# An adaLN block whose first layer norm of groups 2 and 3 is applied to a copy of x laid out by features

## Chip, cores and metric

The kernel runs on one core of one Trainium2 chip. The metric is the device time of one execution in microseconds (us). The time before is 711.41 us, the median of 3 runs (711.18 to 713.69).

## What is computed

A block with adaptive layer norm: sliding-window attention (16 heads of 28, window 256), then a dense layer, Mish, and a dense layer. S = 2048 tokens, D = 448 features, F = 1792.

```python
mod = (silu(c) @ w_mod).reshape(1, 6, 1, 448)      # sa, ca, ga, sb, cb, gb
h = layernorm(x) * (1 + ca) + sa
q, k, v = split(h @ wqkv)                          # 16 heads of 28
p = softmax(mask(q @ k.T / sqrt(28)))              # 0 <= i - j < 256
x = x + ga * ((p @ v) @ wo)
h = layernorm(x) * (1 + cb) + sb
x = x + gb * (mish(h @ w1 + b1) @ w2)
```

## The kernel before

Every matmul operand is split into a high and a low part (hi = value rounded by the write to the matmul type, lo = value - hi), and a product is summed from hi x hi, hi x lo and lo x hi. So each tile that TensorE (PE) makes is evicted twice: ScalarE (ACT) writes hi, VectorE (DVE) writes lo.

The 2048 tokens are four groups of 512 (NG = 4, GT = 512). For each group the first layer norm (L272 to L278, gen_ln at L226) works by tokens: x is loaded with tokens on partitions (x_load, L105), DVE takes mean and variance of each of four tiles (L220, L221), GpSimd (POOL) makes (variance + eps)^-0.5 (L234, L235), DVE subtracts and scales (L241), POOL copies 64 columns once more (dup, L224). Then gen_hT (L287) turns it to features on partitions: four chunks of four PE transposes (L250) into a PSUM buffer "mm", ACT writes hh = chunk * (1 + ca) + sa (L257), DVE makes the same sum in PSUM (L254) and writes hl (L262). From hh and hl come q and k tiles (stored to DRAM through scr) and v.

Attention runs in units. A slot is one head of one group; it has three units, so a group has 48 units: group 0 has units 0 to 47, group 1 has 48 to 95. In unit u (loop at L1026) PE does, in this order: the product of V with Pl of unit u-3 (L741), the scores sB of unit u (L709, L720), score maxima sA for a later slot (L679, reduced by DVE at L681, two PSUM buffers), some filler, and the product of V with Ph of unit u-2. ACT makes P and Ph by exponentials (L723, L724), POOL makes Pl = P - Ph (L731); P, Ph and Pl have three buffers each. The maxima of a pair of slots are transposed (mt, L687), split by DVE (mr, L690) and sent into the q tile by DMA (q<-mr). Every second slot has an et transpose block (L755).

Filler is other work fed to the engines a step at a time by two generators of a group: fill_main (PE work: qkv tiles of this and the next group, the output projection of the group before, gen_hT of the next group) and fill_side (gen_ln1 of the next group, then the preparation of modulation vectors: gen_mod_wo in group 0, gen_mod_ln2 in groups 1 and 2). Each unit adds RATE[g] to a credit and takes filler until it is used up; what is left is drained at the next group's start. The side generator is stepped once per unit; it names "dve" or "act" before a step that uses that engine, and is then passed over in some units (L1064).

All DMAs are issued by SyncE (SP) in one order; a transfer that has to wait for a buffer or for data holds those behind it. DMAs of the filler go into a list, later, from which most units issue one. Every engine works through its own queue in the order of the program.

Of the kernel before, what the change touches and what calls it, by code (L numbers as in the profile page):

```python
# [48 lines left out]


@with_exitstack
def adaln_block(ctx: ExitStack, tc: tile.TileContext, x, wqkv, wo, w1, b1, w2, c, w_mod, out):
# [5 lines left out]
    def dma(o, i):  # L58
        nc.sync.dma_start(o, i)
# [28 lines left out]
    scr = dram.tile([2 * D, 3, S], F32, name="scr")  # L88
    x1d = dram.tile([S, D], F32, name="x1d")
    xnd = dram.tile([NG - 1, GT, 512], F32, name="xnd")  # L90

    def bank(tag, bufs, name):
        return PS[0].tile([128, 512], F32, name=name, tag=tag, bufs=bufs)


    xin = {}

    def x_tile(g):
        xin[g] = qk.tile([128, 4, 512], F32, name=f"xin{g}", tag="xin")

    def x_half(g, t):
        r = g * GT + t * 128
        dma(xin[g][:, t:t + 2, 0:D], xf[r:r + 256, :].rearrange("(t p) d -> p t d", p=128))

    def x_load(g):  # L105
        x_tile(g)
        x_half(g, 0)
        x_half(g, 2)

    x_load(0)  # L110
    wm01 = []
    for k in range(4):
        wmf = st0.tile([128, 2 * D], F32, name=f"wm01_{k}")
# [112 lines left out]
    def gen_ln(tiles, pl, xn_tiles, key, mv=None):  # L226
        if mv is None:
            mv = pl.tile([128, 4, 2], F32, name=f"mv{key}", tag="mv", bufs=2)
            for t in range(4):
                ln_stats(tiles[t], mv[:, t, :], pl, f"{key}{t}")  # L230
                if t < 3:
                    yield
        rs = pl.tile([128, 4], F32, name=f"rs{key}", tag="rs", bufs=2)
        POOL.tensor_scalar(rs, mv[:, :, 1], EPS, None, op0=ALU.add)  # L234
        POOL.tensor_tensor(rs, rs, mhalf, op=ALU.pow)  # L235
        yield
        yield
        xs = xn_tiles()
        for t in range(4):
            xn = xs[t]  # L240
            DVE.tensor_scalar(xn[:, 0:D], tiles[t], mv[:, t, 0:1], rs[:, t:t + 1],  # L241
                              op0=ALU.subtract, op1=ALU.mult)
            if t:
                dup(xs[t - 1])
            yield xs
        dup(xs[3])
# [22 lines left out]
    done = set()  # L269
    XS, HT = {}, {}  # L270

    def gen_ln1(g):  # L272
        def xn_tiles():
            return [xin[g][:, t] for t in range(4)]
        for r in gen_ln([xin[g][:, t, 0:D] for t in range(4)], qk, xn_tiles, f"a{g}"):
            if r:
                XS[g] = r
            yield "dve"  # L278


    def cost(n, cols):
        return n * max(cols / 2200, 0.107)

    pipe = Pipe()
    ht_done = set()

    def gen_hT(g):  # L287
        drain(ln1[g])
        hh, hl = HT[g] = new_T(g, mid)
        for ci in range(4):  # L290
            p = bank("mm", 2, f"tr{g}{ci}")
            tr_chunk(XS[g], ci, p)
            pipe.add(2, lambda p=p, ci=ci: hT_hi(p, ci, hh, 0), lambda p=p, ci=ci: hT_lo(p, ci, hh, hl, 0))
            yield 1.2
        ht_done.add(g)
        if g + 1 < NG:
            loads = (lambda: x_load(g + 1),) if g > 1 else (lambda: (x_tile(g + 1), x_half(g + 1, 0)),
                                                            lambda: x_half(g + 1, 2))
            pipe.add(0, None, None, lambda: later.extend(loads))

    def finish():
        while pipe.items:
            yield
# [1 line left out]
    def drain(*gs):  # L305
        for g in gs:
            for _ in g:
                pipe.step()

    chunk = {"v": 4}  # L310

# [85 lines left out]
    xs0 = XS[0] = [xin[0][:, t] for t in range(4)]  # L397
    for t in range(4):
        ln_stats(xs0[t][:, 0:D], mv0[:, t, :], qk, f"a0{t}")
        if t % 2:  # L400
# [48 lines left out]
    first_split(1)  # L449
    for i in range(2):  # L450
        mod_cols_out(pm[:, 4 * i:4 * i + 4], i)
    hh, hl = HT[0] = new_T(0, mid)
    for ci in range(4):
        hT_hi(trs[ci], ci, hh, 0)
        if ci % 2:
# [40 lines left out]
            for f in qk_out(0, m, p):  # L496
                f()

    x_load(1)
# [25 lines left out]
    wol = [mid.tile([128, D], F32R, name=f"wol_{i}", tag="wo", bufs=7) for i in range(3)]  # L525

    def xr_tile(name):
        return mid.tile([128, 512], F32, name=name, tag="xr", bufs=3)


    def stg(pl, name):
        return pl.tile([128, 512], F32, name=name, tag="stg", bufs=4)

    def wm_load(i, k, pl, ws):
        ws.append(stg(pl, f"wm{i}_{k}")[0:112, 0:D])
# [244 lines left out]
    def lazy(f):  # L780
        yield from f()
# [154 lines left out]
    def fill_main(g):  # L936
        if g == 0:
            yield from gen_qkv(0, VT[:2] + (1,) + VT[2:] + (5, 2, 6))
        else:
            yield from gen_qkv(g, (5, 2, 6))  # L940
            if g == NG - 1:
# [15 lines left out]
    def fill_side(g):  # L957
        if g + 1 < NG:
            yield from ln1[g + 1]
            while g + 1 not in ht_done:  # L960
# [19 lines left out]
    ln1 = {g: gen_ln1(g) for g in range(1, NG)}  # L980
    fillers = {g: fill_main(g) for g in range(NG)}
    side = {g: fill_side(g) for g in range(NG)}

# [3 lines left out]
    def need(keys, g):  # L987
        if all((g, m) in done for m in keys):
            return
        flush()  # L990
        while not all((g, m) in done for m in keys):
            pipe.step()
            try:
# [32 lines left out]
    for u in range(NU + 9):  # L1026
# [27 lines left out]
        if g < NG:  # L1054
            v = u - 48 * g
            if v in (0, 12):
                chunk["v"] = 4 if v == 0 and g or 0 < g < NG - 1 else 2
            if v == 0:
                credit = 0.0
            credit += RATE[g] * (2 if v < FRONT[g] else 1)  # L1060
            while credit > 0.0:
                credit -= step(g)
            if v > 1 or g == 0:
                side_step(g, ("dve", "act")[a >= NS:] if k == 1 else ("act",) if k == 0 and s % 2 == 0 else ())  # L1064
            if later and ((s + (k == 2)) % 2 == 0 or k == 1):
                later.pop(0)()
        if u == NU:
# [111 lines left out]
        st.close()  # L1179


_INS = ["A_x", "A_wqkv", "A_wo", "B_w1", "B_b1", "B_w2", "c", "w_mod"]
_OUTS = [((1, S, D), "float32")]


# [17 lines left out]
```

## Time and profile before

| | |
|---|---|
| runs | 711.41 us median (711.18 to 713.69) |
| profiled execution | 710.72 us |
| its span, first to last instruction | 708.9 us |
| DVE, ACT, POOL busy | 54%, 55%, 46% of the span |
| granted TensorE clock | 0.998 |
| L250 on x (gen_hT) | 48 transposes, from 53.4 to 277.1 us |

The profile is of one execution. Busy is the time in which an engine has an instruction at work; PE's instructions overlap, so PE's place for an instruction is the distance between the starts of two. In rows of the timeline, a bracket tells how long the engine sat idle before the instruction and what ended that. Names are those of the program without buffer numbers; "pv<-Pl" is the product of V with Pl.

The unit at L1026 can be found in the trace by the starts of sB: unit 48 (the start of group 1) starts at 121.6 us, unit 96 at 223.1 us.

### The profile page before, as it was taken

The numbers are of one execution on the slowest core, as the hardware profiler recorded it, in microseconds if no ns is written. First come the engines' busy times: TensorE is split into PE (matmuls) and PEld (weight loads), VectorE is DVE, ScalarE is ACT, GpSimd is POOL, SyncE is SP. The second block draws the span as 40 slices with busy tenths as digits, with TensorE's granted clock in tenths as the row PEclk, the third lists the DMA queues.
The fourth block names the chain that finished last, engine by engine and source line by source line (L and its number), as shares of the span: only waits on it lengthen the run. The fifth ranks groups of instructions, "written<-read, shape, count | busy, mean of one in ns | idle before, by whom it ended". The sixth has DMA issues, their size and how long they took to land.

```text
span 708.9 us, 12034 instructions
## 1 busy us (share of the span) xinstructions
PE 686.6 (97%) x4001; PEld 589.5 (83%) x4001; DVE 385.2 (54%) x1031; ACT 391.1 (55%) x740; POOL 327.0 (46%) x358
## 2 busy tenths in 40 slices
PE   9899999999999999999999799999999999999996
PEld 8677788888898788898887688888888888888885
DVE  5588667688664888555768744351324332532112
ACT  3628778767766858767877874343223322422221
POOL 6626779586766777666778947222010000000002
PEclk9999999999999999999999999999999999999999
DMA  7865764454662462763774155810250035001001
GB/s 211 253 226 181 226 198 150 137 161 150 192 216 66 153 207 76 195 200 92 226 216 128 54 192 166 228 29 1 104 119 1 0 104 119 1 12 41 1 1 52
DMA packets 75178, 90.16 MB, mean 127 GB/s; under 512 B 31535, under 2 KB 51741, under 8 KB 75117
## 3 DMA queue, kind: packets, MB, share of 16 engines
q1 hardware_dynamic: 74652, 89.39, 41.6%
q8 instruction: 32, 0.52, 0.3%
q14 instruction: 30, 0.24, 0.1%
q10 hardware_dynamic: 464, 0.00, 0.0%
HBM read 56.60 MB, written 32.51 MB: 126 GB/s over the span
## 4 chain that ended last, share of the span: by engine, by line
PE 71%; issue 11%; DVE 8%; ACT 2%; DMA 1%; POOL 1%; POOLq 0%; DVEq 0%; ACTq 0%
PE z L912 16%; PE pv L741 9%; PE qk L315 8%; PE sA L679 5%; PE acc L1097 5%; PE acc L1095 5%; PE acc L1096 5%; PE sB L709 5%; PE wo L315 4%; PE qk_v L315 4%; PE sB L720 3%; DVE junk L681 3%; PE et L755 2%; DVE tr L254 1%; ACT P L723 1%
## 5 line engine op out<-in xcount | busy, mean ns | idle before, releaser
L731 POOL TENSOR_TENSOR Pl<-P,Ph 128x512 fp32r<-128x512 f32 (+2 forms) x192 | 234.3, 1227 | 84.3 <-ACT Ph L724 46.1
L681 DVE CUSTOM_DVE_ANT_0 junk<-sA,mask 128x384 f32<-128x384 f32 (+2 forms) x256 | 135.3, 528 | 96.8 <-PE sA L679 88.1
L723 ACT ACTIVATE P<-sB 128x512 f32<-128x512 f32 (+2 forms) x192 | 109.7, 572 | 64.1 <-PE sB L720 59.0
L920 DVE TENSOR_TENSOR al<-t,ah 128x512 fp32r<-128x512 f32 x56 | 38.7, 692 | 178.8 <-ACT ah L919 178.8
L918 ACT ACTIVATE t<-z,b1c 128x512 f32<-128x512 f32 x56 | 38.4, 686 | 165.2 <-PE z L912 161.5
L724 ACT ACTIVATE Ph<-sB 128x512 fp32r<-128x512 f32 (+2 forms) x192 | 109.4, 570 | 0.0
L679 PE MATMUL sA<-k,q 84*128 84x384 f32 (+2 forms) x256 | 100.9, 396 | 2.8 <-DVE mx L681 1.5
L912 PE MATMUL z<-hlf,w 128*128 128x512 f32 x224 | 88.5, 395 | 0.0
L912 PE MATMUL z<-hhf,w 128*128 128x512 f32 x224 | 88.5, 395 | 0.0
L1095 PE MATMUL acc<-w2h,ah 128*128 128x448 f32 x224 | 82.0, 366 | 0.0
L1097 PE MATMUL acc<-w2h,al 128*128 128x448 f32 x224 | 81.9, 366 | 0.0
L1096 PE MATMUL acc<-w2l,ah 128*128 128x448 f32 x224 | 81.5, 364 | 0.0
L741 PE MATMUL pv<-Ph,v 128*60 128x256 f32 (+2 forms) x352 | 76.5, 291 | 3.6 <-DVE o L749 2.3
L741 PE MATMUL pv<-Pl,v 128*60 128x256 f32 (+2 forms) x352 | 73.6, 283 | 2.3 <-POOL Pl L731 2.3
L709 PE MATMUL sB<-q,k 86*128 86x256 f32 (+1 forms) x352 | 74.0, 284 | 0.2 <-DMA q<-mr 0.2
L912 PE MATMUL z<-hhf,w1l 128*128 128x512 f32 x168 | 66.2, 394 | 0.0
L709 PEld LDWEIGHTS sB<-q,k 86*128 86x128 f32 x352 | 61.5, 189 | 1.8 <-issue 0.8
L741 PEld LDWEIGHTS pv<-Ph,v 128*60 128x60 f32 x352 | 45.3, 133 | 18.2 <-ACT o L747 3.2
L720 PE MATMUL sB<-fdmask,identr 128*128 128x128 bf16 (+1 forms) x320 | 60.0, 253 | 0.0
L679 PEld LDWEIGHTS sA<-k,q 84*128 84x128 f32 x256 | 48.9, 192 | 9.1 <-DVE mx L681 6.0
L1106 POOL TENSOR_TENSOR yo<-yo,x 128x448 f32<-128x448 f32 x3 | 3.5, 1211 | 114.9 <-DVE yo L1104 114.9
L741 PEld LDWEIGHTS pv<-Pl,v 128*60 128x60 f32 x352 | 45.0, 131 | 10.8 <-POOL Pl L731 3.9
(161 smaller groups left out, 1291.6 us busy)
## 6 DMA issues: line engine op xcount, KB each, us to landing
scr<-st SPq DMA_DIRECT2D x24, 512.0 KB
k<-scr SPq DMA_DIRECT2D x48, 252.0 KB
q<-scr SPq DMA_DIRECT2D x64, 168.0 KB
scr<-st SPq DMA_DIRECT2D x32, 256.0 KB
x<-x1d SPq DMA_DIRECT2D x10, 448.0 KB
xin<-in_A_x_dram SPq DMA_DIRECT2D x8, 448.0 KB
xr<-in_A_x_dram SPq DMA_DIRECT2D x16, 224.0 KB
x1d<-xr SPq DMA_DIRECT2D x16, 224.0 KB
```

Source lines behind the costliest of these rows:

```text
L315: PE.matmul(p, b, a, start=(n == 0), stop=(n == 10))
L679: PE.matmul(p[:, c0:384], q[0:84, t * 128:(t + 1) * 128], k[0:84, t * 128 + c0:t * 128 + 384], start=True, stop=True)
L681: DVE.tensor_tensor_reduce(out=junk[:, c0:384], in0=p[:, c0:384], in1=mask[:, c0:384], scale=1.0, scalar=-3.0e38, op0=ALU.add, op1=ALU.max ...
L709: PE.matmul(p[:, c:c + 128 * (t1 - t0)], k[:, jj * 128:(jj + 1) * 128], q[:, t0 * 128:t1 * 128], start=(n == 0), stop=False, skip_group_ch ...
L723: ACT.activation(P[:, c0:], p[:, c0:], AF.Exp, scale=SCALE)
L724: ACT.activation(Ph[u][:, c0:], p[:, c0:], AF.Exp, scale=SCALE)
L731: eng.tensor_tensor(Pl[u][:, a:b], Pt[u][:, a:b], Ph[u][:, a:b].bitcast(F32), op=ALU.subtract)
L741: PE.matmul(pv[0:60, t0 * 128:t1 * 128], V[j % NV][:, h, :], P[u][:, c:c + 128 * (t1 - t0)], start=(P is Ph and b == 0 and n == 0), stop=F ...
L912: PE.matmul(zb[n], ps[m][1], ps[m][0], start=(m == 0), stop=(m == 10))
L1095: PE.matmul(p, ah[n][:, ts], w2h[f], start=(f == 0), stop=False)
L1096: PE.matmul(p, ah[n][:, ts], w2l[f], start=False, stop=False)
L1097: PE.matmul(p, al[n][:, ts], w2h[f], start=False, stop=(f == NF - 1))
```

## The change

For groups 2 and 3 the normalised x is no longer transposed by PE. The kernel gets a second input, xt, a copy of x laid out by features, which the host makes before the launch (by moving values, with rows 384 to 447 twice). The statistics still come from x by tokens, in gen_rows: four row tiles, L209 and L210 (L220 and L221 before) on DVE, two small POOL instructions, one PE transpose of the 8 rows of means and factors, a DVE copy, a store to DRAM. gen_x, in the side work of the stage two groups earlier (group 2's in group 0's stage, group 3's in group 1's), reads them back spread over all partitions (two tiles mb of 128x512), loads four chunks of xt, and does chunk - mean on POOL and times factor times (1 + ca) on DVE. gen_ln1, at the beginning of the next stage, adds the shift: hh on ACT, hl on DVE. Group 1 stays as it was (gen_ln1_1, gen_hT1), with four loads of x in place of two.

The tiles hh and hl of the layer norm become tiles of their own, hx and hy; before, they shared buffers with those of the attention output (new_T). The tag stg has 6 buffers (4 before). RATE of groups 1 and 2 goes from 0.91 to 0.83. gen_rows is stepped in the last unit of a slot, and there are more steps of the side work in the last third of groups 0 and 1.

```diff
+    def gen_rows(g):
+        mv = qk.tile([128, 2, 4], F32, name=f"mva{g}", tag="mv", bufs=2)
...
+        for t in range(4):
+            while (g, t) not in sent:
+                yield
+            ln_stats(rows[t], mv[:, :, t], qk, f"a{g}{t}")
+            if t < 2:
+                load(t + 2)
+            yield
+        POOL.tensor_scalar(mv[:, 1], mv[:, 1], EPS, None, op0=ALU.add)
+        POOL.tensor_tensor(mv[:, 1], mv[:, 1], mhalf, op=ALU.pow)
...
+        PE.transpose(p[0:8, 0:128], mv.rearrange("p a t -> p (a t)"), ident)
...
+    def gen_x(g):
...
+        for k in range(4):
+            if k < 2:
+                send((g, "m", k), lambda k=k: dma(mb[k], xms[g - 2, k].rearrange("t p -> (t p)").partition_broadcast(128)))
+            send((g, "x", k), lambda k=k: dma(ys[k], xt[g, k]))
+            yield
...
+        for k in range(5):
+            yield "dve"
+            if k < 4:
+                POOL.tensor_tensor(ys[k], ys[k], mb[0], op=ALU.subtract)
+            if k:
+                DVE.scalar_tensor_tensor(ys[k - 1], ys[k - 1], cols[:, 1, k - 1:k], mb[1],
+                                         op0=ALU.mult, op1=ALU.mult)
...
     def gen_ln1(g):
...
+        while g not in free:
+            yield
+        ys = YS[g]
+        hh, hl = HT[g] = new_H(g)
+        for k in range(5):
             yield "dve"
+            if k < 4:
+                ACT.activation(hh[:, k], ys[k], AF.Identity, bias=cols[:, 0, k:k + 1])
+            if k:
+                DVE.scalar_tensor_tensor(hl[:, k - 1], ys[k - 1], cols[:, 0, k - 1:k],
+                                         hh[:, k - 1].bitcast(F32), op0=ALU.add, op1=ALU.subtract)
+        ready.add(g)
...
-            yield from gen_hT(g + 1)
+            while g + 1 not in ready:
+                yield
...
+            if g + 2 < NG:
+                yield from gen_x(g + 2)
...
-    RATE = {0: 0.56, 1: 0.91, 2: 0.91, 3: 0.65}
+    RATE = {0: 0.56, 1: 0.83, 2: 0.83, 3: 0.65}
...
+            if k == 2 and g < 2 and v >= 3:
+                next(rows[g + 2], None)
+            if g == 0 and k != 1 and u >= 20 or g == 1 and k == 2 and v >= 24:
+                side_step(g)
```

In the changed kernel the lines used below are L345 (POOL's subtraction), L347 (DVE's scaling), L359 (ACT's hh) and L361 (DVE's hl).

PE in unit 71 of group 1, before: tr22 is a chunk of group 2's x, between the et block and the products with V.

```order
L679 MATMUL sA26_3_2610<-k3_2_146,q2_1_459 128x384
L755 MATMUL et10_2613<-ident_132,o2_0_463 128x124 x4
L250 MATMUL tr22_2618<-ident_132,xin2_1112 128x128 x4
L741 MATMUL pv23_2623<-Ph69_2539,v2_167 60x128
L741 MATMUL pv23_2623<-Ph69_2539,v4_169 60x384
```

The same place now; qk2_0 is the first q tile of group 2, made from hx and hy.

```order
L748 MATMUL sA26_3_2666<-k3_2_147,q2_1_465 128x384
L824 MATMUL et10_2669<-ident_133,o2_0_469 128x124 x4
L385 MATMUL qk2_0_2641<-hx2_2157,wql_108 128x512
L385 MATMUL qk2_0_2641<-hy2_2158,wq3_107 128x512
L385 MATMUL qk2_0_2641<-hx2_2157,wq3_107 128x512
L385 MATMUL qk2_0_2641<-hx2_2157,wql_108 128x512
L810 MATMUL pv23_2681<-Ph69_2598,v2_168 60x128
```

The transposes are gone, and group 2's q and k tiles begin four units earlier than before (unit 70 in place of 74).

POOL at the start of group 1, before: Pl53 is of unit 53, rsa2 is the factor of group 2's norm, on0 the attention output.

```order
L731 TENSOR_TENSOR Pl53_2074<-P53_2036,Ph53_2037 128x512
L234 TENSOR_SCALAR rsa2_2086<-mva2_1956 128x4
L235 TENSOR_TENSOR rsa2_2086<-rsa2_2086,mhalf_137 128x4
L731 TENSOR_TENSOR Pl54_2102<-P54_2070,Ph54_2071 128x512
L771 TENSOR_TENSOR on0_972<-ol7_2081,rc7_2107 128x4x56
L773 COPY on0_972<-on0_972 128x4x64
L731 TENSOR_TENSOR Pl55_2140<-P55_2098,Ph55_2099 128x512
```

The same place now.

```order
L800 TENSOR_TENSOR Pl53_2111<-P53_2076,Ph53_2077 128x512
L800 TENSOR_TENSOR Pl54_2139<-P54_2107,Ph54_2108 128x512
L840 TENSOR_TENSOR on0_988<-ol7_2118,rc7_2144 128x4x56
L842 COPY on0_988<-on0_988 128x4x64
L800 TENSOR_TENSOR Pl55_2180<-P55_2135,Ph55_2136 128x512
```

The two instructions of the norm no longer stand between Pl53 and Pl54.

POOL near the end of group 1, before: Pl88 to Pl92 with one on between.

```order
L731 TENSOR_TENSOR Pl88_3147<-P88_3111,Ph88_3112 128x512
L731 TENSOR_TENSOR Pl89_3183<-P89_3143,Ph89_3144 128x512
L731 TENSOR_TENSOR Pl90_3213<-P90_3179,Ph90_3180 128x512
L771 TENSOR_TENSOR on1_2299<-ol13_3190,rc13_3218 128x4x56
L731 TENSOR_TENSOR Pl91_3244<-P91_3209,Ph91_3210 128x512
L731 TENSOR_TENSOR Pl92_3267<-P92_3240,Ph92_3241 128x512
```

The same place now; xt3_0 to xt3_3 are group 3's chunks, mb3_0 its means.

```order
L800 TENSOR_TENSOR Pl88_3213<-P88_3174,Ph88_3175 128x512
L345 TENSOR_TENSOR xt3_0_2954<-xt3_0_2954,mb3_0_2952 128x512
L345 TENSOR_TENSOR xt3_1_2955<-xt3_1_2955,mb3_0_2952 128x512
L800 TENSOR_TENSOR Pl89_3244<-P89_3209,Ph89_3210 128x512
L345 TENSOR_TENSOR xt3_2_2956<-xt3_2_2956,mb3_0_2952 128x512
L800 TENSOR_TENSOR Pl90_3273<-P90_3240,Ph90_3241 128x512
L840 TENSOR_TENSOR on1_2345<-ol13_3251,rc13_3278 128x4x56
L800 TENSOR_TENSOR Pl91_3303<-P91_3269,Ph91_3270 128x512
L345 TENSOR_TENSOR xt3_3_2957<-xt3_3_2957,mb3_0_2952 128x512
L800 TENSOR_TENSOR Pl92_3329<-P92_3299,Ph92_3300 128x512
```

Four instructions of the size of a Pl stand among five Pl. In group 0's end the four of group 2 stand in the same way: one ahead of Pl44, two ahead of Pl45, one ahead of Pl47. PE's last qk_v matmul of group 1's filler stands in unit 92 now and in unit 94 before, so units 93 to 95 have no filler.

More of the change, by code (lines that the diff above doesn't have):

```diff
@@ new lines, in adaln_block @@
+    YS = {}
+    def gen_x(g):
+        while (g, 4) not in sent:
+            next(rows[g], None)
+            yield
+        yield
+        yield
+        mb = [stg(qk, f"mb{g}_{a}") for a in range(2)]
+        ys = [stg(qk, f"xt{g}_{k}") for k in range(4)]
+        for k in range(4):
+            if k < 2:
+                send((g, "m", k), lambda k=k: dma(mb[k], xms[g - 2, k].rearrange("t p -> (t p)").partition_broadcast(128)))
+            send((g, "x", k), lambda k=k: dma(ys[k], xt[g, k]))
+            yield
+        while (g, "x", 3) not in sent:
+            yield
+        for k in range(5):
+            yield "dve"
+            if k < 4:
[3 more added lines that the diff above has]
+                                         op0=ALU.mult, op1=ALU.mult)
+        YS[g] = ys
@@ L396, in adaln_block @@
     rs0 = st0.tile([128, 2, 4], F32, name="rs0")
-    xs0 = XS[0] = [xin[0][:, t] for t in range(4)]
+    xs0 = XS[0] = [xin0[:, t] for t in range(4)]
     for t in range(4):
@@ L992, in need @@
             pipe.step()
+            if g not in ready:
+                next(side[max(g - 1, 0)], None)
             try:
@@ L1192 @@
     arrays, args = {}, []
+    rows = [*range(D), *range(384, D)]
+    xt = _np.asarray(inputs["A_x"])[0].T[rows].reshape(4, 128, NG, GT).transpose(2, 0, 1, 3)
+    inputs = {**inputs, "xt": xt}
     for name in _INS:
```

97 lines of the change are left out of this document (58 added, 39 removed).

## The prediction

> **What bounds the kernel now.** I read the page first, for the engine that carries the end.
>
> ```profile
> span 708.9 us, 12034 instructions
> PE 686.6 (97%) x4001; PEld 589.5 (83%) x4001; DVE 385.2 (54%) x1031; ACT 391.1 (55%) x740; POOL 327.0 (46%) x358
> PE 71%; issue 11%; DVE 8%; ACT 2%; DMA 1%; POOL 1%; POOLq 0%; DVEq 0%; ACTq 0%
> ```
>
> PE is busy 97% of the span and holds 71% of the chain that ended last. What the change can give is matmul work taken out, and waits of PE that go. Both lie in the attention stage, so next came the busy time by windows, here the first half of group 1.
>
> ```profile
> core 0: us, PE busy (x) PEld busy (x) DVE busy (x) ACT busy (x) POOL busy (x), PEclk, DMA share, GB/s
> 142.00:152.00 10.00, 9.54 (x68) 8.33 (x67) 8.61 (x22) 7.27 (x15) 8.62 (x10) 1.00 0.67 209
> 172.00:182.00 10.00, 9.33 (x65) 8.01 (x66) 9.08 (x25) 8.06 (x16) 7.08 (x7) 1.00 0.34 96
> 182.00:192.00 10.00, 10.00 (x69) 8.56 (x68) 5.24 (x17) 7.36 (x15) 6.62 (x6) 1.00 0.85 249
> ```
>
> The clock is full. PE is full from 182 on, and loses time in two places: at the start of the group, where DVE and POOL stand at 8.6 of 10 us, and at 172 to 182, where DVE is at 9.1. The second place is where group 2's normalised x is transposed. Group 2 repeats both places 102 us later. Last came the timeline at the two places.
>
> **The change part by part, against the profiled execution (710.7 us, span 708.9).**
>
> *Transposes that go.* Groups 2 and 3 lose 2 x 4 chunks of four transposes each (L250). The timeline of PE around three of the chunks:
>
> ```profile
> 169.50 0.60 PE L250 MATMUL tr<-ident,xin 128*128 128x128 f32 x4
> ...
> 169.86 0.42 PE L679 MATMUL sA<-k,q 84*128 84x384 f32 x1
> ...
> 171.19 0.59 PE L755 MATMUL et<-ident,o 124*128 124x124 f32 x4
> ...
> 172.58 0.63 PE L250 MATMUL tr<-ident,xin 128*128 128x128 f32 x4 [0.81 <-DVE hl L262]
> ...
> 222.17 0.59 PE L755 MATMUL et<-ident,o 124*128 124x124 f32 x4
> 222.52 0.47 PE L741 MATMUL pv<-Ph,v 128*60 128x128 f32 x2
> ```
>
> A chunk lasts 0.60 us, but the next matmul starts 0.36 us after it (169.50 to 169.86): that is its place on PE. 8 x 0.36 = **-2.9 us**. One of these chunks in each group finds its PSUM buffer not yet emptied. After an et block the next matmul normally starts 0.35 us later (222.17 to 222.52); here it took 1.39. 1.04 us go, twice: **-2.1 us**. DVE is freed there of 4 L254 and 4 L262 at 0.82 and 0.69 us (rows below), so I also take off 0.3 us per group of its late evictions: **-0.6 us**, an estimate between 0 and the 0.67 us of idle that the 172 to 182 row shows.
>
> The Trainium skill's "TensorE: Matmul & The Clock Gate" (Part 4: PE-mode transpose) gives about 275 ns for a transpose inside a kernel; 32 of them would be 8.8 us and the sum below 5.9 us lower. The rows show the same duration but not that price, since four overlap.
>
> *The norm's start that goes.* In groups 1 and 2, L234 waits in POOL's queue for the last L221, and L235 follows; the subtraction Pl that PE needs stands behind them.
>
> ```profile
> 138.77 0.23 POOL L234 TENSOR_SCALAR rsa<-mva 128x4 f32<-128x4 f32 x1 [1.23 <-DVE mva L221]
> 139.09 1.04 POOL L235 TENSOR_TENSOR rsa<-rsa,mhalf 128x4 f32<-128x4 f32 x1
> 140.11 1.28 POOL L731 TENSOR_TENSOR Pl<-P,Ph 128x512 fp32r<-128x512 f32 x1
> ...
> 140.72 0.44 PE L741 MATMUL pv<-Ph,v 128*60 128x128 f32 x2
> 141.44 0.45 PE L741 MATMUL pv<-Pl,v 128*60 128x128 f32 x2 [0.28 <-POOL Pl L731]
> ...
> 142.33 0.27 PE L687 MATMUL mt<-ident,mx 128*8 128x128 f32 x1
> 142.44 0.60 PE L250 MATMUL ot<-ident,on 128*128 128x128 f32 x4
> 142.79 0.48 PE L741 MATMUL pv<-Ph,v 128*60 128x256 f32 x2
> 143.67 0.45 PE L741 MATMUL pv<-Pl,v 128*60 128x256 f32 x2 [0.40 <-POOL Pl L731]
> ...
> 145.11 0.40 PE L741 MATMUL pv<-Ph,v 128*60 128x128 f32 x2
> 145.35 0.40 PE L741 MATMUL pv<-Pl,v 128*60 128x128 f32 x2
> ```
>
> The step from Ph to Pl takes 0.24 us when nothing waits (145.11 to 145.35); twice here it takes 0.72 and 0.88. The 1.1 us are lost in each of the two groups: **-2.2 us**. In the new order the two small POOL instructions of group 2 are off this place (they move into the middle of group 0, those of group 3 into the middle of group 1), and the dup copies go too. What takes the place: 4 ACT instructions (L359) and 4 DVE instructions (L361) per group, right where ACT also evicts the ot tiles. ACT and DVE lose their L241, L254, L257 and L262 elsewhere:
>
> ```profile
> L241 DVE TENSOR_SCALAR xin<-xin,mva,rsa 128x448 f32<-128x448 f32 x4 | 4.6, 1143 | 0.0
> L254 DVE TENSOR_SCALAR tr<-tr,cols 128x512 f32<-128x512 f32 x4 | 3.3, 816 | 0.0
> L257 ACT ACTIVATE hh<-tr,cols 128x512 fp32r<-128x512 f32 x4 | 3.2, 796 | 0.4 <-PE tr L250 0.4
> L262 DVE TENSOR_TENSOR hl<-tr,hh 128x512 fp32r<-128x512 f32 x4 | 2.8, 692 | 0.1
> L175 DVE SCALAR_TENSOR_TENSOR wm<-wm,sT,wm x12: 678/681/1415, 79.8 to 342.8; 112x448 f32<-112x448 f32 x12
> ```
>
> ACT: 4 x 0.80 = 3.2 us in a place where it is busy 7.3 of 10; its PE cost lies between 0 and 3.2. DVE's new L347 and L361 have the form of L175: 0.68 to 1.42 us for 448 columns, 0.78 to 1.62 scaled to 512; I take 0.95, nearer the median. Per group DVE drops 4.6 + 3.3 + 2.8 = 10.7 and gets 8 x 0.95 = 7.6. I give back 0.2 us in group 2, and 0.4 in group 1 where group 3's statistics now also fall: **+0.6 us**. The two transposes of the means cost as much as the mt block above (142.33 to 142.44): **+0.2 us**.
>
> *POOL at the ends of groups 0 and 1.* The four new subtractions (L345) of 128x512 have the form of Pl, 1.29 us. In group 1's order they stand among Pl88 to Pl92.
>
> ```profile
> 207.43 1.29 POOL L731 TENSOR_TENSOR Pl<-P,Ph 128x512 fp32r<-128x512 f32 x1 [0.42 <-ACT Ph L724]
> ...
> 215.06 0.56 POOL L771 TENSOR_TENSOR on<-ol,rc 128x224 f32<-128x224 f32 x1 [1.07 <-ACT Ph L724]
> ...
> 221.34 0.40 PE L741 MATMUL pv<-Pl,v 128*60 128x128 f32 x2
> ...
> 209.59 0.77 PE mc L180 x8
> 211.56 1.43 PE qk_v L315 x7
> ```
>
> The first row is Pl88; it ends at 208.7. PE wants Pl92 at 221.3, 12.6 us later. From Pl88's end to Pl92's, POOL now has 4 subtractions, 4 Pl and one on: 8 x 1.29 + 0.56 = 10.9 us. But PE gets there sooner: between the same points it loses 15 qk_v matmuls, which the new rate puts earlier (29 stand in these units before and 14 now; seven take 1.43 us in the last row, from the chain, so 0.205 each), and the mc block, 0.77. That is 3.9 us less, so Pl92 is wanted 8.7 us after and comes 2.2 us late. Packed Pl start somewhat closer than 1.29, so **+1.9 us**, between 0 and 2.2. DVE stands behind too: the last L347 waits for the last subtraction, with the sA evictions queued behind it, and PE's third sA waits for those; that stall ends at the same time and is not added.
>
> At the end of group 0 the subtractions meet shorter Pl, and the four POOL instructions L569, 4.7 us there before, have moved ahead:
>
> ```profile
> L569 POOL TENSOR_TENSOR wop<-wop,ga 128x448 f32<-128x448 f32 x4 | 4.7, 1164 | 0.0
> L220 DVE BATCH_NORM_STATS2 sta<-xin 128x6 f32<-128x448 f32 x16 | 9.9, 617 | 3.5 <-DMA xin<-in_A_x_dram 3.3
> ```
>
> Three of them precede the Pl that PE wants next: 0 if the vacated time takes them, 3.9 if not; I take **+0.7 us**, since 5.2 replace 4.7. Group 2's statistics, 4 x 0.62 = 2.5 us of DVE and four small L221, move into group 0's middle: between 0 (while DVE has room, the evictions are not late) and 2.5, I take **+0.6 us**.
>
> *DMA.* SP gets 22 issues in place of 4 for groups 2 and 3, and 4 for 2 in group 1. Each takes about 0.4 us of a queue that mostly waits (the last row is the wait at 108 us, for group 0's end):
>
> ```profile
> SPq L59 <- DVE mr L690: 149.6, 29, 10.7
> 206.99 0.41 SPq L59 DMA_DIRECT2D q<-scr  x1
> SPq L59 <- DVE mr L690: 1.9, 1, 1.9
> ```
>
> So I price them at nothing; the cover is SP's waiting, and without it 20 x 0.4 = 8 us would fall on the q and k loads. The one new wait that can stand on SP, the read of the means behind their store, comes several slots after it.
>
> **Sum:** -2.9 - 2.1 - 0.6 - 2.2 + 0.6 + 0.2 + 1.9 + 0.7 + 0.6 = **-3.8 us**, 706.9 for this execution. The median of the runs shown is 711.4, 0.7 above it, so I forecast **707.6 us**, 0.5% faster. About 0.5%, 3.6 us, is also what a measurement of this kernel can tell from no change.
>
> **The rivals.**
>
> *All waits go and none come.* If POOL's and DVE's new work at the two group ends hides, +0.6, +1.9, +0.7 and +0.6 fall away: -7.6, **704 us**. For it: POOL is busy only 46% of the span. Against it: the replay at Pl92.
>
> *The new work gives back the gain.* ACT and DVE at the starts cost 2 x 1.5 in place of 0.6, group 0's end 1.5, its statistics 1.5 (each about half of its upper bound) and Pl92 2.2: -3.8 + 2.4 + 0.8 + 0.9 + 0.3 gives +0.6, **712 us** at worst, 710 to 712 in all. For it: DVE at 9.1 of 10 us in these places before, and L241 took 1143 ns on average while POOL worked, so the new DVE instructions may be as stretched. The Trainium skill's "SBUF — State Buffer" (Who interferes with whom) states the mechanism: a DVE instruction with two SBUF inputs and a GpSimd instruction that reads SBUF block each other outright. L347 and L361 have two; the L254 and L262 that go had at most one. By this rule alone each of the 16 could stand for a whole Pl, by estimate up to 16 x 1.29 = 20.6 us more of DVE, and the kernel would be slower than before. L175 also has two such inputs, and its median of 681 ns with a largest of 1415 shows that the full stand is rare here; I give it 0.08 of this case's 0.22.
>
> *SP makes it slower.* The chunks xt3_2 and xt3_3 are issued behind the q<-mr of the pair before, and SP stands at such waits for up to 10.7 us (row above). If that wait is longer than the two units between issue and use, about 4 us (a unit is 102 / 48 = 2.1), POOL's third subtraction stands for the landing, Pl90 and all behind it stand too, and PE stops with them. A wait at its longest, 10.7, less 4, gives +6.7 us: -3.8 + 6.7 = +2.9 at one group end, and if both ends do it +9.6, **714 to 721 us**. Against it: group 0's chunks stand ahead of the next q<-mr, and SP's wait there was 1.9 us.
>
> **How the numbers follow.** Forecast 0.47 (its own range 705.5 to 709.5: the +1.9 and +0.7 terms at either end), all waits gone 0.22, new work gives back 0.22, SP 0.09. The forecast lies on the line of 0.5%, and I count two thirds of it as faster: 0.31 + 0.22 = 0.53 faster; slower 0.09 + 0.01 = 0.10; same 0.37. The range for 8 in 10 reaches from below the all-gone case, 702.5, to the dear end of the give-back case, 712.
>
> **What would show it.** Right: no L250 on group 2's or 3's x; the Ph to Pl steps at the start of groups 1 and 2 back at about 0.24 us; PE waiting for Pl by 1 to 2 us within the last four units of group 1, none in group 2's end, which has no subtractions. Wrong: PE waits for sA evictions in the middle of group 0 of over 1.5 us; POOL's L345 idle until a DMA; L347 or L361 over 1.2 us on average; a time under 704 would say that POOL's replay is too dear, one over 711 that the starts kept their waits.

## The result, and the profile after

The changed kernel takes 723.17 us (median of 4 runs, 721.26 to 724.20), the kernel before 712.00 beside it: ratio 1.0151, 95% interval 1.0121 to 1.0181. It is slower by 11 us, where 707.6 and "faster" were forecast and 712 was the upper end of the range. The profiled run took 724.2 us (span 722.4). The profile's page, the counterpart of the three lines shown of before:

```profile
span 722.4 us, 12014 instructions
PE 690.5 (96%) x3971; PEld 590.4 (82%) x3971; DVE 386.3 (53%) x1025; ACT 390.2 (54%) x740; POOL 340.8 (47%) x358
PE 63%; issue 18%; DVE 9%; DMA 4%; POOL 3%; ACT 2%; SPq 1%; POOLq 0%; DVEq 0%; ACTq 0%
```

PE has 30 matmuls fewer (32 transposes out, two in) and is busy 3.9 us longer. DVE is busy 1 us longer, POOL 14 us, and neither comes near to full. So the loss is neither PE's work nor an engine that is full; PE stands, and it runs slowly. Where, is read from the starts of the units: the time from one unit's first sB matmul to that of a later unit, in us, from the rows of PE in the traces (runs with work left out are explained below).

| units | before | after | no arithmetic | also no extra calls | last version |
|---|---|---|---|---|---|
| 12 to 14 | 2.8 | 3.5 | 3.5 | 3.5 | 3.5 |
| 22 to 36 | 23.1 | 26.4 | 27.3 | 23.4 | 22.7 |
| 47 to 49 (end of group 0) | 4.3 | 9.9 | 4.5 | 4.5 | 5.1 |
| 54 to 64 (start of group 1) | 19.8 | 19.9 | 19.8 | 19.8 | 20.8 |
| 92 to 96 (end of group 1) | 7.8 | 11.7 | 7.2 | 5.9 | 5.9 |
| 48 to 96 (group 1) | 101.5 | 108.8 | 102.3 | 101.2 | 99.1 |
| 96 to 144 (group 2) | 101.8 | 98.6 | 98.4 | 98.3 | 99.4 |

Group 2, which has no statistics and no subtractions in it, is 3.3 us shorter: the gains that were forecast are there. Groups 0 and 1 lose 7.7 and 7.3 us, and group 3 another 2.0 in this execution, of which 1.7 are a low clock (last section). The largest loss in one place is at the end of group 0. Its timeline in the profile of after, DVE, POOL and the first PE instruction that waits:

```profile
122.20 0.76 DVE L347 SCALAR_TENSOR_TENSOR xt<-xt,cols,mb 128x512 f32<-128x512 f32 x1
122.37 2.95 POOL L345 TENSOR_TENSOR xt<-xt,mb 128x512 f32<-128x512 f32 x2
124.13 1.74 DVE L347 SCALAR_TENSOR_TENSOR xt<-xt,cols,mb 128x512 f32<-128x512 f32 x1 [1.18 <-POOL xt L345]
125.79 0.55 DVE L750 CUSTOM_DVE_ANT_0 junk<-sA,mask 128x384 f32<-128x384 f32 x1
126.40 0.69 PE L748 MATMUL sA<-k,q 84*128 84x384 f32 x1 [2.58 <-DVE mx L750]
...
130.25 0.63 PE L385 MATMUL qk<-hx,wql 128*128 128x512 f32 x1
130.68 0.63 PE L385 MATMUL qk<-hy,wq 128*128 128x512 f32 x1
...
133.65 0.40 PE L385 MATMUL qk<-hy,wq 128*128 128x512 f32 x1
133.89 0.40 PE L385 MATMUL qk<-hx,wq 128*128 128x512 f32 x1
```

The first L347 takes 0.76 us. The second stands 1.18 us for POOL's subtraction and then takes 1.74 us for the same work. Only then comes the sA eviction (L750), and PE has stood for 2.58 us. After that one projection matmul follows the other every 0.43 us (130.25 to 130.68) where it is 0.24 us three microseconds later (133.65 to 133.89). The windows show why, in the column PEclk (third from the right):

```profile
124.00:126.00 2.00, 0.00 (x0) 0.00 (x0) 1.87 (x2) 1.01 (x3) 2.00 (x3) 0.90 0.44 119
126.00:128.00 2.00, 1.60 (x6) 1.46 (x7) 1.71 (x7) 0.00 (x0) 2.00 (x3) 0.50 0.72 252
128.00:130.00 2.00, 2.00 (x9) 1.71 (x8) 2.00 (x2) 0.74 (x2) 2.00 (x2) 0.50 0.16 61
130.00:132.00 2.00, 2.00 (x7) 1.52 (x6) 1.88 (x4) 1.14 (x3) 1.36 (x2) 0.50 0.00 0
132.00:134.00 2.00, 2.00 (x12) 1.67 (x11) 0.15 (x1) 0.26 (x1) 0.25 (x1) 0.90 0.00 0
...
234.00:236.00 2.00, 2.00 (x11) 1.45 (x12) 1.82 (x7) 1.03 (x2) 1.73 (x2) 0.70 0.01 2
236.00:238.00 2.00, 2.00 (x11) 1.80 (x9) 0.63 (x4) 0.65 (x2) 1.22 (x1) 0.50 0.66 165
238.00:240.00 2.00, 2.00 (x12) 1.73 (x11) 0.57 (x2) 1.34 (x3) 0.28 (x2) 0.94 0.84 258
```

The granted clock halves in the last 0.8 us of the stand (0.90 in the first row). From 126.4 to 132.4 PE gets half speed, 3.0 us lost; 2.58 + 3.0 = 5.6 us is the whole loss of units 47 to 49. At the end of group 1 a stand of 2.5 us is followed by (0.30 + 0.50 + 0.06) x 2 = 1.7 us.

What makes the second L347 long is seen best where DVE waits for no result of POOL's. In group 1 of the profile of after, a DVE and a POOL instruction begin together, twice:

```profile
162.53 1.28 POOL L800 TENSOR_TENSOR Pl<-P,Ph 128x512 fp32r<-128x512 f32 x1 [1.08 <-ACT Ph L793]
162.58 1.79 DVE L361 SCALAR_TENSOR_TENSOR hy<-xt,cols,hx 128x512 fp32r<-128x512 f32 x1
...
164.29 0.62 DVE L209 BATCH_NORM_STATS2 sta<-xr 128x6 f32<-128x448 f32 x1
164.29 1.29 POOL L800 TENSOR_TENSOR Pl<-P,Ph 128x512 fp32r<-128x512 f32 x1 [0.47 <-ACT Ph L793]
```

L361 reads two tensors from SBUF. It begins 0.05 us behind Pl and ends 0.56 us after Pl's end, most of its own 0.73 us: it ran for the most part when Pl was done. L209 reads one tensor and takes its usual 0.62 us beside a Pl. The groups of the instructions (minimum/median/maximum in ns):

```profile
L347 DVE SCALAR_TENSOR_TENSOR xt<-xt,cols,mb x8: 760/1621/1759, 122.2 to 231.6; 128x512 f32<-128x512 f32 x8
L361 DVE SCALAR_TENSOR_TENSOR hy<-xt,cols,hx x8: 729/748/1793, 152.2 to 270.3; 128x512 fp32r<-128x512 f32 x8
L345 POOL TENSOR_TENSOR xt<-xt,mb x8: 1256/1282/1727, 119.9 to 230.3; 128x512 f32<-128x512 f32 x8
```

It cuts both ways: L345 and Pl take 1.73 us where an L347 had begun before them (1.28 + 0.45). L347 is hit nearly always. Three of the eight are released at the very moment when L345 ends and POOL begins its next instruction, and take 1.74, 1.75 and 1.74 us; most of the others find POOL in the middle of an instruction.

The theory, then: (B) a DVE instruction with two SBUF inputs and a POOL instruction run one after the other, so L347 holds DVE's queue for 1.6 us and the sA evictions behind it are late; the stand of PE costs again through the clock. The rivals: (A) the wait of L347 for L345 in DVE's queue is the cause, not its stretch; (C) the statistics and what else was moved into the middle of groups 0 and 1.

### The profile page after: what moved, and what is told of

Its sections match the earlier page's. It is cut to its first block, busy times and chain, and to the rows that moved or that the text cites. A ratio compares the mean times of both kernels' runs of the same rounds, so it can differ in the third digit from the quotient of the medians.

```text
span 722.4 us, 12014 instructions
## 1 busy us (share of the span) xinstructions
PE 690.5 (96%) x3971; PEld 590.4 (82%) x3971; DVE 386.3 (53%) x1025; ACT 390.2 (54%) x740; POOL 340.8 (47%) x358
## 4 chain that ended last, share of the span: by engine, by line
PE 63%; issue 18%; DVE 9%; DMA 4%; POOL 3%; ACT 2%; SPq 1%; POOLq 0%; DVEq 0%; ACTq 0%
PE z L981 12%; PE pv L810 8%; PE qk L385 7%; PE sA L748 5%; PE sB L778 4%; PE wo L385 4%; PE acc L1179 4%; PE acc L1177 4%; PE acc L1178 4%; PE qk_v L385 3%; PE sB L789 3%; DVE junk L750 3%; PE et L824 2%; DMA xr<-in_A_x_dram 2%; PE warm L498 1%
## 5 line engine op out<-in xcount | busy, mean ns | idle before, releaser
L800 POOL TENSOR_TENSOR Pl<-P,Ph 128x512 fp32r<-128x512 f32 (+2 forms) x192 | 238.0, 1245 | 87.2 <-ACT Ph L793 54.7
L750 DVE CUSTOM_DVE_ANT_0 junk<-sA,mask 128x384 f32<-128x384 f32 (+2 forms) x256 | 135.0, 527 | 98.6 <-PE sA L748 89.5
L748 PE MATMUL sA<-k,q 84*128 84x384 f32 (+2 forms) x256 | 101.3, 398 | 13.1 <-DVE mx L750 12.4
```

The source lines that it names most:

```text
L748: PE.matmul(p[:, c0:384], q[0:84, t * 128:(t + 1) * 128], k[0:84, t * 128 + c0:t * 128 + 384], start=True, stop=True)
L750: DVE.tensor_tensor_reduce(out=junk[:, c0:384], in0=p[:, c0:384], in1=mask[:, c0:384], scale=1.0, scalar=-3.0e38, op0=ALU.add, op1=ALU.max ...
L800: eng.tensor_tensor(Pl[u][:, a:b], Pt[u][:, a:b], Ph[u][:, a:b].bitcast(F32), op=ALU.subtract)
```

## The experiments

All times are medians beside the kernel before on the same chip (711.5 to 712.2 us); ratios are to it.

**What the arithmetic costs.** The loop with L345 and L347 is taken out.

```
-        for k in range(5):
-            yield "dve"
-            if k < 4: POOL.tensor_tensor(...)              # L345
-            if k: DVE.scalar_tensor_tensor(...)            # L347
```

> Leaves out the work of L345 and L347 in both group ends (8 subtractions, 8 scalings); the chunks are still loaded and used raw. Theory A (the loss sits at the two group ends: DVE stands in L347 behind POOL's L345, the sA evictions behind it are late, PE stands 2.5 to 2.9 us and then runs at a granted clock of 0.5 for 2 to 6 us): units 47 and 48 last 1.65 and 2.7 us again in place of 5.5 and 4.4, units 93 to 95 last 3.5 to 5 us together in place of 9.1, no slice below a clock of 0.95, and the time falls by 10 to 12 us, to 711 to 713. Rival C (the loss comes from the row statistics, their loads and the earlier mod work in the middle of groups 0 and 1): the time stays above 717.

714.33 us, ratio 1.0035 (1.0021 to 1.0049): 8.8 us less than after, where 10 to 12 were expected. The two group ends come back as expected (table, fourth column) and the clock holds. But units 22 to 36 stay 4 us too long, so the group ends are not all.

**The wait taken away, the shared access kept.** `POOL.tensor_tensor` of L345 becomes `DVE.tensor_tensor`.

> All work done; L345 moves from POOL to DVE, so L347 never waits for POOL. Theory A, by the wait: the waits of L347 for POOL (4.6 us in all) go, DVE gets 8 x 0.7 = 5.6 us more of its own work; PE's stands at the group ends shrink under 1.5 us, the clock holds, 714 to 718. Theory B (a DVE instruction with two SBUF inputs and a POOL instruction that reads SBUF don't run at the same time, which is why L347 takes 1.62 us in the middle against 0.76 at least): the 16 DVE instructions still meet POOL's Pl, each stretched to up to 1.6 us, 720 to 726.

727.39 us, ratio 1.0207 (1.0179 to 1.0235). L347 waits for POOL nowhere and still has a median of 1.48 us; the subtractions on DVE take 0.68 to 0.69 us where POOL rests or begins after them, and 1.30 to 1.36 where Pl has begun before. PE's stands grow to 3.7 and 3.4 us, and each is followed by 6.3 us of half clock. So the loss doesn't need the wait for POOL. That theory A is wrong isn't shown by this run alone, since DVE's queue now holds 7.4 us of subtractions more at the same places.

**The wait made shorter.** L347 two steps behind L345.

```
-        for k in range(5):
+        for k in range(6):
...
-            if k:          # L347 on chunk k - 1
+            if k > 1:      # L347 on chunk k - 2
```

> All work done; each L347 stands two steps of the side work behind its L345 in place of one. Theory A, by the wait: L347 finds its input ready nearly always (waits of 4.6 us go to under 1), the gap of PE at the end of group 0 falls from 2.9 to under 2 us, no slice below a clock of 0.9: 715 to 719. Theory B: L347 still takes 1.5 us or more in the middle and holds the sA evictions as long as before, 721 to 724.

722.60 us, ratio 1.0149 (1.0119 to 1.0180), the same as after within the intervals. L347's waits for POOL fall only from 4.6 to 2.9 us, and its median from 1.62 to 1.10. In its profile the stand at the end of group 0 is 1.99 us and no low clock follows, so units 47 to 49 take 6.5 us; at the end of group 1 a low clock comes behind a stand of 1.07 us. In both stands PE waits for Pl, no longer for an sA eviction: with DVE's queue freed, POOL's replay, which the prediction had priced, shows behind it. The theories are not told apart by this run.

**What the statistics cost.** `ln_stats` of groups 2 and 3 is taken out.

```
-            ln_stats(rows[t], mv[:, :, t], qk, f"a{g}{t}")
+            if t == 0:
+                POOL.memset(mv[:, :, :], 1.0)
```

> Leaves out the row statistics of groups 2 and 3 (L209 and L210 of xr, 8 each; the means and variances are set to one value); their loads, the transpose of the means and all that follows stay. Rival C: 3 to 5 us of the loss goes, units 13, 22 to 23, 65 to 68 come back, 718 to 720. Theory A alone: under 1.5 us, 721.5 or more, and both group ends keep their low clock.

719.13 us, ratio 1.0102 (1.0082 to 1.0122): 4.0 us less than after. Rival C holds for this part, and the group ends keep their stands of 2.6 and 2.5 us. In group 1 the statistics cost more than their time because they fall among wo's residual adds and because DVE waits in front of one of them (profile of after):

```profile
172.19 0.63 DVE L209 BATCH_NORM_STATS2 sta<-xr 128x6 f32<-128x448 f32 x1 [2.84 <-DMA xr<-in_A_x_dram]
...
173.40 0.61 DVE L710 TENSOR_TENSOR xr<-xr,wo 128x448 f32<-128x448 f32 x1
173.54 0.44 PE L748 MATMUL sA<-k,q 84*128 84x384 f32 x1 [0.34 <-DVE mx L750]
175.40 0.44 PE L748 MATMUL sA<-k,q 84*128 84x384 f32 x1 [0.53 <-DVE mx L750]
```

**The shared access taken away, the wait kept.** In L347's place stands a statistics instruction that reads the chunk alone.

```
-                DVE.scalar_tensor_tensor(ys[k - 1], ys[k - 1], cols[:, 1, k - 1:k], mb[1], ...)
+                DVE.bn_stats(st, ys[k - 1])
```

> Leaves out the scaling by the inverse deviation: in L347's place stands, at the same point of DVE's order and behind the same L345, a statistics instruction that reads the chunk alone (one SBUF input; the like of it, L209, took 0.62 us beside Pl in the profile of after). Theory B (the shared access): it takes about 0.7 us each time whether POOL runs or not, no POOL instruction there takes 1.7 us any more, PE's gap at the end of group 0 falls from 2.6 to under 2 us, the clock holds, 714 to 718 us, although DVE still waits for L345. Theory A (the wait in DVE's queue alone): DVE's waits for L345 stay at 3 us or more and PE's gaps at 2.3 to 2.9 us with their low clock, 719 to 723 us.

715.71 us, ratio 1.0062 (1.0036 to 1.0088): 7.5 of the 8.8 us are gone. The group of the stand-in, of L345, and the stand-in's waits:

```profile
L348 DVE BATCH_NORM_STATS2 sx<-xt x8: 672/694/695, 123.8 to 226.3; 128x6 f32<-128x512 f32 x8
...
  POOL xt L345: 5.2, 4
...
L345 POOL TENSOR_TENSOR xt<-xt,mb x8: 1258/1282/1290, 121.5 to 225.0; 128x512 f32<-128x512 f32 x8
```

DVE waits for L345 longer than in after (5.2 against 4.6 us), but nothing is stretched, on either engine. At the end of group 0 PE's longest stand is 1.1 us and the clock holds. At the end of group 1 two stands of 0.96 and 0.82 us, 1.5 us apart, still bring 6.8 us of half clock in the profiled execution, which took 718.4 us. The first is, by the profile, for a load of k and is there without the arithmetic too (1.07 us in the first experiment); the second is for an sA eviction behind a stand-in that had waited 2.4 us for L345. The windows:

```profile
226.00:228.00 2.00, 1.18 (x7) 0.82 (x6) 1.62 (x6) 1.08 (x2) 2.00 (x3) 0.81 0.00 0
228.00:230.00 2.00, 2.00 (x11) 1.68 (x10) 1.58 (x6) 0.62 (x2) 2.00 (x2) 0.50 0.02 4
```

The stand-in differs from L347 in a second way: it writes 6 columns in place of 512. That this isn't the reason is seen at L409 in the profile of after. It writes 128x512 to SBUF from one input in PSUM and one in SBUF, and takes 0.67 to 0.69 us in all 12 cases in which it begins while a POOL instruction of 128x512 is at work. So theory B holds: with the same wait and no stretch, the median keeps 1.4 of the 8.8 us. A small rest, and a low clock in some executions, stay with the wait.

**The clock by itself.** The kernel before, with DVE held at four places.

```
             B(u)
+            for n in range({40: 4, 88: 6, 136: 8, 160: 10}.get(u, 0)):
+                DVE.bn_stats(junk[:, 0:6], mask)
```

> The kernel before with DVE held on purpose at four places: 4, 6, 8 and 10 statistics instructions of about 0.55 us on the mask (results unused), in units 40, 88, 136 and 160, so that the sA evictions behind them are 2.2, 3.3, 4.4 and 5.5 us late and PE stands about 1 us less each time. Theory of the clock: the first gap costs itself alone, at the two longest the granted clock falls to about 0.5 for 2 to 6 us behind the gap and each costs 2 to 3 us above its length; the second tells where the limit lies; 725 to 731 us in all. Rival (a gap costs its length, the low clock came from something else): clock 1.00 throughout, 720 to 723 us.

731.90 us, ratio 1.0276 (1.0251 to 1.0301), a little above what the theory of the clock gave. PE's stands are 1.84, 1.71, 2.89 and 4.73 us. The third of them in windows:

```profile
320.00:322.00 2.00, 2.00 (x14) 1.94 (x13) 1.46 (x5) 0.00 (x0) 0.00 (x0) 0.87 0.99 332
322.00:324.00 2.00, 2.00 (x11) 1.77 (x11) 0.37 (x3) 0.00 (x0) 0.00 (x0) 0.50 0.88 265
324.00:326.00 2.00, 2.00 (x9) 1.87 (x8) 0.57 (x2) 1.33 (x3) 0.14 (x1) 0.50 0.04 12
326.00:328.00 2.00, 2.00 (x8) 1.71 (x8) 0.00 (x0) 0.54 (x1) 1.14 (x1) 0.50 0.00 0
328.00:330.00 2.00, 2.00 (x14) 1.80 (x13) 0.99 (x5) 1.08 (x2) 0.03 (x1) 0.92 0.00 0
```

Summed over such windows, the half clock costs 0, 1.7, 3.4 and 1.6 us behind the four. Stand and clock together are the loss: units 88 to 92 take 3.5 us longer (1.71 + 1.7), 128 to 141 6.2 (2.89 + 3.4), 160 to 172 6.2 (4.73 + 1.6). So a stand brings on the low clock, with nothing but DVE's delay changed. A limit in length is not there: 1.71 us brought it on, 1.84 didn't (the last section has what the traces show of this).

**The extra calls.** The first experiment again, also without the line that was put into the loop over the units.

```
-            if g == 0 and k != 1 and u >= 20 or g == 1 and k == 2 and v >= 24:
-                side_step(g)
```

> Leaves out the work of L345 and L347 as the first experiment did (714.3 us), and also the line that calls the side work an extra time per unit in the last third of groups 0 and 1, so that the wm scalings (L164) and the wop products (L638) spread out again. If the bunching of this side work costs PE the 2 to 3 us that units 22 to 36 lost with and without the arithmetic: those units together back from 26.3 to under 24.5 us, 711 to 712.5 us. Rival (the extra calls cost nothing, the loss comes from the statistics and the means' transposes): 713.8 to 715 us.

708.95 us, ratio 0.9951 (0.9937 to 0.9966): 5.4 us less than the first experiment, and more than expected. Units 22 to 36 fall from 27.3 to 23.4 us and 92 to 96 from 7.2 to 5.9. The windows of after and of this run over the first part, from 74 to 84 us:

```profile
74.00:84.00 10.00, 8.60 (x56) 6.52 (x55) 8.52 (x26) 7.71 (x18) 8.26 (x9) 1.00 0.47 141
```

```profile
74.00:84.00 10.00, 10.00 (x67) 8.10 (x65) 8.55 (x31) 7.99 (x19) 7.97 (x9) 1.00 0.60 165
```

The same side work (the L164 scalings), called once more in two units of three, comes in a bunch in front of the sA evictions, and PE loses 1.4 of 10 us. L164 has two inputs in SBUF too; in after the first of the three is stretched and the other two follow 0.6 us behind its end (first two rows), in this run they are spread out (last two):

```profile
79.58 1.42 DVE L164 SCALAR_TENSOR_TENSOR wm<-wm,sT,wm 112x448 f32<-112x448 f32 x1
81.64 1.76 DVE L164 SCALAR_TENSOR_TENSOR wm<-wm,sT,wm 112x448 f32<-112x448 f32 x2
```

```profile
80.57 0.71 DVE L164 SCALAR_TENSOR_TENSOR wm<-wm,sT,wm 112x448 f32<-112x448 f32 x1
83.32 0.68 DVE L164 SCALAR_TENSOR_TENSOR wm<-wm,sT,wm 112x448 f32<-112x448 f32 x1
```

**The arithmetic moved to the next group's start.** Its loop stands ahead of `gen_ln1`'s wait, the loads stay, the extra calls go, the last two statistics of each group wait one step longer.

> All work done. The chunks are loaded where they were, but L345 and L347 move to the start of the next group (groups 1 and 2), where PE has 4 to 8 filler matmuls per unit and POOL and DVE stand at 3 to 4 of 6 us; the extra side steps go; the statistics of rows 2 and 3 wait one step longer for their loads. If what costs is a stretched DVE instruction where PE has no cover: units 47 to 49 and 92 to 96 come back to 4.5 and under 8 us, 708.5 to 712 us. Rival (the pairs cost the same wherever they stand): the starts of groups 1 and 2 each lose 3 to 5 us, 716 to 720 us.

716.87 us, ratio 1.0059 (1.0038 to 1.0081), the rival's time. But the units tell more than the sum: in units 49 to 57 nothing is lost; units 58 and 59, with the last pair, take 7.7 us where 4.5 do without the arithmetic (the seventh experiment), about the same in group 2. Of these 3.2 us 1.7 are half clock, though no stand there is over 0.8 us. And a low clock behind a stand of 1.7 us in unit 65 costs 1.7.

**All three taken out.**

> Leaves out the work of L345 and L347, the row statistics L209 and L210 of groups 2 and 3, and the extra calls of the side work: all three costs that the runs so far priced at 8.9 (arithmetic), 4.0 (statistics) and 5.4 us (extra calls). If these three are the whole loss and add up: 723.2 - 8.9 - 4.0 - 5.4 = 704.9, so 704 to 706 us, which is also the forecast's sum with its three costs at nothing (711.4 - 7.6 + 0.2 = 704). Rival (they overlap, or something else is lost too): 707 to 709 us.

706.01 us (704.35 to 709.29), ratio 0.9910 (0.9890 to 0.9929). Arithmetic 8.8, extra calls 5.4 and statistics 2.9 (708.95 to 706.01; 4.0 in the presence of the others) make 17.1 us. They add up to the way from 723.2 because they were taken off one after the other; the test is the expected 704.9, from prices of runs with the other costs in place, of which 1.1 us are missing. The profiled execution, the longest of the five (709.3), has one more loss: DVE waits 2.7 us in front of a residual add, by the profile for a DMA, PE stands 2.4 us at unit 71, and 1.7 us of half clock follow. What remains is about the forecast's case in which no new wait costs anything, 704.

**A pair in every unit.** `yield "dve"` becomes `yield` in the moved loop, and group 3's statistics begin at the 21st unit of group 1's stage.

```
-            if k == 2 and g < 2 and v >= 3:
+            if (k == 2 and g == 0 and v >= 3) or (k != 1 and g == 1 and v >= 21):
                 next(rows[g + 2], None)
```

> All work done. As the run with the arithmetic at the group start (716.9 us), where the first three pairs cost nothing and the fourth, at units 58 and 59, cost 3.2 us in each group; now a pair in every unit, so that all four stand in units 51 to 55, ahead of the evictions of the transposed attention output. Group 3's statistics move from units 56 to 70 to units 70 to 80, off the residual adds of wo. If the loss depends on where the pairs meet DVE's other work: units 54 to 64 back to 19.9 us, 64 to 70 to under 13 us, 707 to 711 us. Rival (a pair costs 1 us or more anywhere): 713 to 717 us.

716.01 us, ratio 1.0065 (1.0050 to 1.0079). The statistics' part came out as expected (units 64 to 70 take 12.4 us, 14.6 in after). The pairs' part didn't: units 54 to 64 take 24.2 us. The timeline of this run there (its L352 is L347, its L411 the eviction L409, its L239 the attention output's transposes):

```profile
142.86 1.74 DVE L352 SCALAR_TENSOR_TENSOR xt<-xt,cols,mb 128x512 f32<-128x512 f32 x1 [0.32 <-POOL xt L350]
144.52 0.55 DVE L752 CUSTOM_DVE_ANT_0 junk<-sA,mask 128x384 f32<-128x384 f32 x1
145.00 0.68 DVE L411 TENSOR_TENSOR st<-qk,st 128x512 fp32r<-128x512 f32 x1
145.73 1.08 PE L239 MATMUL ot<-ident,on 128*128 128x128 f32 x4 [3.06 <-DVE st L411]
```

Two stretched L347 delay the eviction of the last q/k block, whose PSUM buffer the next ot chunk needs: a stand of 3.06 us and 1.7 us of half clock, in both groups.

**Two units earlier.** In the loop over the units, on top of that:

```
-            if v > 1 or g == 0:
+            if v > 1 or g == 0 or g < 3 and v >= 0:
                 side_step(...)
```

> All work done. As the run before, with the pairs two more units ahead (units 48 to 53), where PE has 7 to 8 filler matmuls per unit in place of 4. By the theory of cover it is as fast or up to 1 us faster than that run, 706.5 to 711 us; if POOL's first subtraction there waits for the chunks' loads, which are issued only at the group's boundary, Pl is late and it is 2 to 4 us slower than that run.

708.38 us (707.53 to 709.41), ratio 0.9957 (0.9943 to 0.9972). All work is done, and this beats both kernels. The same pair in this run's timeline, and the PE rows next to it:

```profile
135.27 1.76 DVE L352 SCALAR_TENSOR_TENSOR xt<-xt,cols,mb 128x512 f32<-128x512 f32 x1 [0.70 <-POOL xt L350]
136.44 1.73 POOL L350 TENSOR_TENSOR xt<-xt,mb 128x512 f32<-128x512 f32 x1
136.96 0.54 DVE L752 CUSTOM_DVE_ANT_0 junk<-sA,mask 128x384 f32<-128x384 f32 x1
137.56 0.45 PE L750 MATMUL sA<-k,q 84*128 84x384 f32 x1
```

L347 is as stretched as ever (1.25 to 1.77 us, all eight), but between the two sA matmuls around this pair (134.91 and 137.56) PE has the et block, four projections, PV and scores to do, and hardly stands. Units 54 to 64 take 20.8 us. Of the 8.8 and 2.9 us of the arithmetic and the statistics, 708.38 - 706.01 = 2.4 us are left.

## Why the prediction was wrong

- **Transposes, buffer wait, norm's start (-2.9, -2.1, -0.6, -2.2): right in sum.** 3.9 us of these per group, less 0.2 given back, were to fall to group 2; it is 3.3 us shorter. Of the parts only the norm's start is seen by itself: units 49 to 54 are 1.1 us shorter, as forecast. And with all new costs out the kernel takes 706.0, where 704 was worked out for "all waits go".
- **L347 and L361 at 0.95 us: mis-sized.** L347 takes 1.44 on average, over the 1.2 that was to show the prediction wrong, and L361 1.03. A value near the median of L175 was taken. But in the profile of before only four of the twelve L175 began while a POOL instruction of 128x512 was at work, and these took 0.72 to 1.42 us, the other eight 0.68. The sentence that the full stand is rare was read from the wrong kind of row. The rule of the Trainium skill's "SBUF — State Buffer" (Who interferes with whom) is the one that decides, and had 0.08: by it a DVE instruction with two SBUF inputs and a GpSimd instruction that reads SBUF take turns. The fifth experiment agrees, with 0.69 us for one input and no stretch on POOL; that each of the 16 stands for a whole Pl did not come, since five of the eight L361 took 0.73 to 0.75 us.
- **"That stall ends at the same time and is not added": the step that failed.** POOL's replay to Pl92 was priced at +1.9 and the end of group 0 at +0.7, with DVE's queue taken as hidden behind Pl at the end of group 1 and not counted at all at the end of group 0. It was the other way round: Pl hardly kept PE waiting (0.4 us), sA behind L347 did, 2.58 and 2.50 us. Only when L347 was moved back did PE stand for Pl (1.99 and 1.07 us, third experiment). Units 47 to 49 lost 5.6 us, and the arithmetic 8.8 us in all, against 2.6.
- **The clock: missing.** No term of the sum had it; 3.0 and 1.7 us of the two group ends in the profile of after are low clock. The Trainium skill's "TensorE: Matmul & The Clock Gate" (Part 1: The HAM clock gate) gives half speed after an idle window of about 3.4 us and full speed after a busy one. The low stretches here agree in length (3.4 us or about twice that); stands of 1.7 to 2.9 us were enough, and in the third and fifth experiments single ones of about 1 us, which is shorter than the page's window.
- **The extra calls: priced at nothing, 5.4 us.** The diff's line was read as what makes room for the new work. It moved all side work from unit 20 of group 0 on, and the bunch met DVE ahead of the sA evictions.
- **Group 0's statistics (+0.6): right in size** (0.7 at units 12 to 14, gone without them). Group 3's, counted within +0.4, cost about 2.7 us (units 64 to 79 take 35.3 us in after and 32.6 without the statistics): the load that DVE waits for was not looked for.
- **DMAs (0), and the SP rival at 0.09: right.** No L345 waited for a load in after, and the issues on SP cost nothing that a run shows; the load that L209 waits for is counted with the statistics.

## What to carry to other kernels

Before adding a DVE instruction, ask what stands behind it in DVE's queue, how long it is with POOL beside it if it reads two SBUF tensors, and how many matmuls PE has until it needs what stands behind. Stands of PE of 1.7 to 2.9 us cost up to about twice their length here (2.58 + 3.0 us, 2.89 + 3.4), so work that may hold an eviction belongs where PE's queue is fullest, not where the engine that does it is idlest. Of side work that is called more often, price all that it carries forward.

## What the runs showed of the hardware

- The low clock comes in portions: about 3.4 us at half speed (1.7 us lost) or about twice that. The portions begin on a grid: in the profile of after at 125.6, 234.8 and 419.1 us (0.90, 0.70 and 0.78 in the windows above and below), 32 and 54 steps of 3.41 us apart, and in each of the other profiles that have several they are whole steps of 3.41 us apart too. So it matters how a stand falls on the steps. All kernels have a stand of 2.3 us at the end of the attention stage (PV waits for DVE's o). The windows behind it, in after and in before:

```profile
418.00:420.00 2.00, 0.98 (x5) 0.88 (x6) 1.94 (x4) 0.62 (x2) 1.23 (x2) 0.78 0.00 0
420.00:422.00 2.00, 2.00 (x12) 1.81 (x11) 0.09 (x1) 1.07 (x2) 0.00 (x0) 0.50 0.00 0
```

```profile
406.00:408.00 2.00, 0.76 (x7) 0.67 (x7) 1.94 (x4) 0.84 (x2) 1.45 (x2) 1.00 0.00 0
408.00:410.00 2.00, 2.00 (x19) 1.67 (x18) 0.70 (x3) 1.56 (x4) 0.34 (x1) 1.00 0.00 0
```

  The same stand was followed by the low clock in 10 of the 13 profiles, not in those of before, of the first experiment and of the last version. By PE's rows, the ten have a step in which PE has no matmul at work for 1.79 to 2.29 us; in the other three the stand falls on two steps, with at most 1.18, 1.70 and 1.32 us in one. From 20 us to the end of the attention stage every step with 1.73 us or more was followed by the low clock; from 1.04 to 1.70 us it came out both ways, and what decides there stays open. Part of the spread between runs of one kernel is this: of the eight runs of the fifth experiment, the four with a mean granted clock of 0.998 took 713.7 to 715.3 us, the four with 0.989 to 0.993 716.1 to 720.2.
- Some DVE instructions with one SBUF input are stretched too: in the profile of before, the four L241 of group 1 take 1.20, 1.38, 0.50 and 1.49 us, the three long ones where a Pl had begun before them. L209, also with one input, never is.
